# 374 kept rows instead of 372, the last folded group in two pieces of three rows, and a longer round through the small places

## The chip, the cores and the metric

The kernel runs on one core of one Trainium2 chip. The metric is the device time of one execution in microseconds (us); times are compared as medians of several runs on the same chip.

## The reference

The input `x` is an image of 384 x 384 pixels with 384 channels in bf16 (113.25 MB), `w1d` is a single weight. Each channel is averaged over all pixels, the average is weighted and goes through a sigmoid, and the whole image is multiplied by the result, channel by channel:

```python
B, H, W, C = x.shape
g = jnp.einsum("bhwc->bc", x) / (H * W)
s = jnp.zeros_like(g)
for i in range(k):                     # k = 1
    s = s + gp[:, i:i + C] * w1d[i]    # gp: g, padded by k // 2 = 0
s = _sigmoid(s)
return x * s[:, None, None, :]
```

All of `x` has to be read before the first element of the output is known, and all of it has to be written.

## The kernel before

**Rows and passes.** The image is seen as 128 partitions of 1152 rows; a row is one pixel's 384 channels in one partition, 768 bytes, so one row over all partitions is 98,304 bytes. The first pass (summing) loads all 1152 rows; TensorE multiplies each row by a matrix of ones and adds it to one PSUM bank, so that the bank holds the channels' sums in all partitions (`sum_rows`, L291). ScalarE makes the scale `s_bf` of it (L503) and puts a copy into the bank (L507, `s_ps`). The second pass (scaling) multiplies and stores all rows. A row that is still in SBUF then need not be read again. Rows that are not kept are called streamed: they are loaded, summed, and overwritten, and are loaded a second time for the scaling.

**Places.** SBUF holds an arena of 275 rows (`ROWS`). More rows than that are kept, by folding: four rows of bf16 values in the usual range of exponents fit into three. `fold` (L331) works on a piece of `p` rows of each of four parts: VectorE shifts and masks the fourth row's bits into temporary rows at `T` and joins them into free exponent bits of the other three; ScalarE looks at test values at `Y`, and records in `seen` whether a value was out of range (then GpSimd does those rows again at the end, `again`, L608). A group `(a, q)` holds 4q rows: 3q folded rows from `a` on, and behind them q "top" rows that become free when the group is folded. There is a first group of 4, two columns of four groups of eight, one group of six whose folded rows are copied into PSUM banks (`BANKED`), and a last one (`EXTRA`) of four at `A` (220). The rows that are kept unfolded ("raw") take the places that remain: the tops of the two columns' last groups (`U`, rows 108 to 115, and `V`, 212 to 219), the rows from `W` (232) on, and the rows `T` (259) and `Y` (267) to 274. `N_RAW`, `N_STREAM` and the runs of rows in DRAM follow from these (from L199 on).

**The summing pass.** A list (`BETWEEN`, L466) gives for each group which places the streamed rows between it and the next pass through. Large places of 48 rows come first; toward the end the places get smaller, since the arena fills with kept rows. Behind the last group, `EXTRA`, come four places of 8, 8, 8 and 7 rows (`LATE`, L465): `W + 4`, `U`, `W + 12`, `W + 20`, one load each. The raw rows come last (L495): `V`, again `LATE`, then `W`, `T`, `Y` in loads of 8 to 2 rows. A load into a place waits until TensorE has summed what was there. The number of rows in the second load of the whole pass is what the rest leaves over (`left % 48`, L474).

**Queues.** SyncE issues all loads and stores, in the order in which the program adds them; an issue waits for its semaphores, and everything behind it on SyncE waits with it. The transfers themselves are worked off in this order. `Flow` (L21) works out the waits. `hold` repeats a wait n times without work; `N_DVE` and `N_SP` (L371) say how often VectorE (at the start, and before the first scale) and SyncE do this.

**The scaling pass.** Its order is planned when the program is built, by a loop (L771) that plays VectorE and the queue through with assumed durations, and so decides which rows are scaled, stored, loaded and unfolded next. The places of raw rows are scaled first, in the order in which they stand in `landed` (L692 to L695); three pieces at the end of the rows behind `W` are scaled by GpSimd alongside (L701), and until GpSimd is thought to be done the planner starts no unfolding and lets VectorE read the scale from the bank. Then groups are unfolded in the order `order` (L707): per piece VectorE takes the fourth row's bits out (three `bits`, two `join`: L315, L321), restores the three rows, and scales. Rows whose store has landed become places for streamed rows.

Of the kernel before, what the change touches and what calls it, by code (L numbers as in the profile page):

```python
# [145 lines left out]
def kernel(  # L146
# [12 lines left out]
    P = nc.NUM_PARTITIONS  # L159
    B, H, W, C = x.shape  # L160
    (k,) = w1d.shape
    assert k == 1 and B == 1
    HW = H * W
    RPP = HW // P
# [7 lines left out]
    PIECE = 4  # L172
    PAIR = 2 * PIECE
    PAIRS = 4
    U = 3 * PIECE + PAIRS * 3 * PAIR
    G0 = U + PAIR
    V = G0 + PAIRS * 3 * PAIR
    A = V + PAIR
    N_A = 39
    T = A + N_A  # L180
    Y = T + 2 * PIECE
# [3 lines left out]
    FIRST = 0  # L185
    GROUPS = [(0, PIECE)]
    COLUMNS = ([FIRST], [])
    for i in range(PAIRS):
        for column, a in zip(COLUMNS, (3 * PIECE, G0)):
            column.append(len(GROUPS))  # L190
            GROUPS.append((a + 3 * PAIR * i, PAIR))
    BANKED = len(GROUPS)
    GROUPS.append((A, 6))
    EXTRA = len(GROUPS)
    GROUPS.append((A, PIECE))
    W = A + 3 * PIECE
    PS = 3 * GROUPS[BANKED][1]
    N_BANKED = 4 * GROUPS[BANKED][1] + 1
    N_RAW = ROWS - W + 2 * PAIR  # L199
    pool = ctx.enter_context(tc.tile_pool(name="sb", bufs=1))  # L200
# [1 line left out]

    pieces = [
        (g, lo, min(m, q - lo))
        for g, (_, q) in enumerate(GROUPS) for m in [q if g == BANKED else PIECE] for lo in range(0, q, m)
    ]

    ones = pool.tile([P, P], bf16, name="ones")
# [45 lines left out]
    for g, (_, q) in enumerate(GROUPS):  # L254
        c_group.append(N_STREAM if g == BANKED else r)
        r += 0 if g == BANKED else 4 * q
    c_raw = r
    assert c_raw + N_RAW == RPP

    def raw(a):  # L260

        return c_raw + (a - U if a < G0 else PAIR + a - V if a < A else 2 * PAIR + a - W)

# [3 lines left out]
    def load(at, a, n):  # L267

        r0, m = run = run_of(at)
        lo, hi = at - r0, at - r0 + n  # L270
        assert hi <= m
        fl.add(
            "SP",
            lambda: nc.sync.dma_start(out=arena[:, a : a + hi - lo, :], in_=view(xf, *run)[:, lo:hi, :]),  # L274
            writes=rows(a, hi - lo), dma=True,
        )
# [91 lines left out]
            join(w2, w2, flat(T + i * p, p), XOR, wc[2] + rows(T + i * p, p), wc[2])  # L368


    N_DVE, N_SP = (62, 14), 20  # L371

    fl.add("ACT", lambda: nc.scalar.dma_start(out=w_bf[:], in_=w1d.to_broadcast((1, 1))), writes=["w_bf"], dma=True)
    fl.add("DVE", lambda: nc.vector.memset(ones[:], 1.0), writes=["ones"])  # L374
# [25 lines left out]
    def stream_all(where, n=None):  # L400
        i = 0
        n = sum(m for _, m in where) if n is None else n
        while n:
            a, m = where[i % len(where)]
            m = min(n, m)
            stream(m, a)
            n -= m
            i += 1

    def take(g, lo=0, hi=None):  # L410

        a, q = GROUPS[g]
        hi = (N_BANKED if g == BANKED else 4 * q) if hi is None else hi
        load(c_group[g] + lo, a + lo, hi - lo)
        return sum_rows(a + lo, hi - lo)

    def of_group(g):
        return [i for i, piece in enumerate(pieces) if piece[0] == g]
# [13 lines left out]
    for i, bk in enumerate(banks):  # L432
        lo, hi = i * BANK, min((i + 1) * BANK, PS * C)
# [4 lines left out]
    S1, S2, S3 = ([slot] for slot in SLOTS)  # L438
# [9 lines left out]
    def group(g, where):  # L448

        if isinstance(where, list):  # L450
            take(g)
            for k in of_group(g):
                fold(k)
            stream_all(where)
        else:
            k1, k2 = of_group(g)
            take(g, 0, 12)
            take(g, 24, 32)
            fold(k1)
            stream_all(where[0])  # L460
            take(g, 12, 24)
            fold(k2)
            stream_all(where[1])

    LATE = [(W + 4, 8), (U, 8), (W + 12, 8), (W + 20, 7)]  # L465
    BETWEEN = [  # L466
        (2, LOW_COLUMN + HIGH), (4, [(A, 38)]),
        (5, [(G0 - 24, 24), (A - 24, 24), *S1]),
        (6, (S2, S3 + S1)), (7, ([(A - 24, 24)] + S2, S3 + S1)),
        (8, (S2 + S1, [(U, 8)] + S3)), (EXTRA, LATE),  # L470
    ]
    between = sum(n for _, b in BETWEEN for w in b for _, n in (w if isinstance(w, list) else [w]))
    first = N_STREAM - between
# [18 lines left out]
        load(raw(a), a, n)  # L492
        return sum_rows(a, n)

    for a, n in [(V, 8), *LATE, (W, 4), (T, 4), (T + 4, 4), (Y, 4), (Y + 4, 2), (Y + 6, 2)]:  # L495
        step = take_raw(a, n)
        if a == Y - 4:
            fl.hold("DVE", 2 * N_DVE[1], step)
# [144 lines left out]
    landed = deque()  # L643
# [45 lines left out]
        return f  # L689


    for a, n, end in ((Y, 2, True), (Y + 2, 2, True), (Y + 4, 4, True), (U, 4, True), (U + 4, 4, True), (T, 8, True), (V, 8, True)):  # L692
        landed.append((a, raw(a), n, end))
    landed.append((W, raw(W), 8, True))
    landed.append((W + 8, raw(W + 8), 6, True))  # L695


    alongside = deque()
    t = 1.0
    for a, n in ((A + 26, 4), (A + 30, 4), (A + 34, 5)):  # L700
        scale(a, n, "POOL", after=[copied])  # L701
        t += 0.2 + 0.84 * n
        alongside.append((t, a, raw(a), n))


    (c0, c1), N_NEAR = COLUMNS, 2
    order = [c0[-1], EXTRA, c0[-2], c1[-1], BANKED, c0[-3], c1[-2], c0[-4], c1[-3], FIRST, c1[-4]]  # L707
    line = deque(order)
    home = {g: i for i, column in enumerate(COLUMNS) for g in column}
    home[BANKED], home[EXTRA] = 2, 3  # L710
# [60 lines left out]
    while True:  # L771

        if dve_at <= now:
# [4 lines left out]
            if landed and (ahead < PENDING or not can):  # L778
                a, at, n, end = landed.popleft()
# [13 lines left out]
        if alongside and alongside[0][0] <= now:  # L793
            _, a, at, n = alongside.popleft()
# [3 lines left out]
        while waiting and waiting[0][0] <= now:  # L798
            _, n, then, at, a, known = waiting.popleft()
# [10 lines left out]
        if bank_at is None and len(line) <= total - BANKS_AT and got and max(got)[0] >= N_BANKED:  # L810
            a = max(got)[1]
# [3 lines left out]
            for i, bk in enumerate(banks):  # L815
                lo, hi = i * BANK, min((i + 1) * BANK, PS * C)
# [6 lines left out]
        if got and todo < N_STREAM:  # L823
            n, a = max(got)
            left = N_STREAM - todo
            left -= run_of(left - 1)[0]
            n = min(n, CAP, left)
            ahead = backlog()
            behind = storing and sum(m for m, _ in got) < MANY and ahead >= SHORT
            if not behind and (todo or not (landed or alongside or waiting)) and (n >= min(BIG, left) and (n == left or left > CAP) or (ahead < LOW and n >= 8) or ahead < LAST):  # L830
                storing = False

                lo = N_STREAM - todo - n
# [51 lines left out]
```

## Time and profile before

| | us |
|---|---|
| median of 3 runs | 719.24 |
| lowest and highest | 718.77, 719.40 |
| the profiled execution's own time | 718.83 |
| its span, first to last instruction | 717.1 |

The page shows one execution. Its engines: TensorE busy 213.0 us, VectorE 475.2, ScalarE 121.4, GpSimd 10.2. In the fences, PE is TensorE, DVE VectorE, ACT ScalarE, POOL GpSimd, SP SyncE (SPq its issues of transfers); L517 is a line of the kernel. In a view in order of time, a row has the start, the duration, the engine, the line, the operation with its shape, how often it stands there, and in brackets the idle time before it and what ended that. In the views of transfers stand the size of one and the median time from issue to landing, so a wait in the queue is part of it. The summing pass ends near 268 us, and the first store is issued at 269.8.

### The profile page before, as it was taken

How to read it: one execution, taken by the hardware profiler on the slowest of the kernel's cores; microseconds unless marked ns; L12 is line 12 of the kernel's file. 1: busy time of each engine (PE TensorE's matmuls, PEld its weight loads, DVE VectorE, ACT ScalarE, POOL GpSimd, SP SyncE). 2: the span in 40 equal slices, each digit the busy share in tenths (PEclk: the TensorE clock that was granted, in tenths of full speed). 3: DMA queues.
4: the chain of work that ended last, by engine and by line, in shares of the span. 5: the costliest groups of instructions: out<-in, count | busy, mean ns of one | idle time of the engine just before them, and what ended most of it. 6: DMA issues, size and time to landing. Idle time of an engine off the chain costs nothing.

```text
span 717.1 us, 2040 instructions
## 1 busy us (share of the span) xinstructions
PE 213.0 (30%) x1186; PEld 0.3 (0%) x3; DVE 475.2 (66%) x355; ACT 121.4 (17%) x97; POOL 10.2 (1%) x7
## 2 busy tenths in 40 slices
PE   4776978998869780000000000000000000000000
PEld 0000000000000000000000000000000000000000
DVE  4606280639896829999999999779966960128900
ACT  3704160426674610000110000000000000000000
POOL 0000000000000005000000000000000000000000
PEclk9998989999999996555555555555555555555555
DMA  9999999999999989999999999999999999999997
GB/s 373 436 426 440 424 442 426 439 429 420 428 430 425 427 358 355 406 424 431 433 428 422 444 424 445 423 439 428 439 420 435 433 433 436 436 432 431 437 421 343
DMA packets 21038, 303.31 MB, mean 423 GB/s; under 512 B 2338, under 2 KB 2850, under 8 KB 9378
## 3 DMA queue, kind: packets, MB, share of 16 engines
q1 hardware_dynamic: 21024, 303.18, 99.1%
q8 instruction: 4, 0.07, 0.0%
q14 instruction: 8, 0.07, 0.0%
q10 hardware_dynamic: 2, 0.00, 0.0%
HBM read 189.92 MB, written 113.25 MB: 423 GB/s over the span
## 4 chain that ended last, share of the span: by engine, by line
DMA 56%; DVE 23%; PE 7%; another core or an unknown queue 3%; ACT 2%; POOL 1%; SPq 1%; issue 0%; DVEq 0%
DMA arena<-in_x_dram 45%; DVE arena L517 17%; DMA out_dram<-arena 11%; PE bank L280 7%; DVE arena L315 4%; ACT arena L352 2%; DVE arena L321 2%; POOL arena L517 1%; SPq L274 1%; SPq L531 0%; ACT s_bf L503 0%; ACT bank L507 0%; ACT bank L429 0%; DVEq L124 0%
## 5 line engine op out<-in xcount | busy, mean ns | idle before, releaser
L517 DVE TENSOR_TENSOR arena<-arena,s_bf 128x6144 bf16<-128x6144 bf16 (+13 forms) x67 | 226.9, 3424 | 86.1 <-DMA arena<-in_x_dram 71.0
L280 PE MATMUL bank<-arena,ones 128*128 128x384 bf16 x1151 | 207.2, 342 | 46.2 <-DMA arena<-in_x_dram 45.6
L315 DVE TENSOR_SCALAR arena<-arena 128x1536 uint16<-128x1536 uint16 (+4 forms) x193 | 136.9, 763 | 107.6 <-DMA arena<-in_x_dram 94.9
L352 ACT ACTIVATE arena<-arena 128x3072 uint16<-128x3072 uint16 (+1 forms) x38 | 107.6, 2831 | 111.6 <-DVE arena L315 111.6
L321 DVE TENSOR_TENSOR arena<-arena 128x1536 uint16<-128x1536 uint16 (+3 forms) x81 | 106.3, 1312 | 8.4 <-PE bank L280 5.2
L597 PE MATMUL bank<-odd,ones 128*128 128x1 bf16 x1 | 0.2, 184 | 262.2 <-DVE odd L592 262.2
L429 ACT COPY arena<-bank 128x512 uint32<-128x512 uint32 (+3 forms) x9 | 4.4, 497 | 86.6 <-DMA out_dram<-arena 86.3
L517 POOL TENSOR_TENSOR arena<-arena,s_bf 128x1536 bf16<-128x1536 bf16 (+1 forms) x3 | 9.9, 3345 | 269.2 <-ACT bank L507 269.2
L517 DVE TENSOR_TENSOR arena<-arena,bank 128x1536 bf16<-128x1536 bf16 (+3 forms) x8 | 9.4, 1248 | 0.0
L429 ACT COPY bank<-arena 128x512 uint32<-128x512 uint32 (+3 forms) x9 | 4.1, 489 | 26.5 <-PE bank L280 26.5
L352 ACT ACTIVATION_READ_ACCUMULATOR arena<-arena 128x1 f32 x38 | 7.1, 186 | 0.0
L280 PE MATMUL bank<-zeros,ones 128*128 128x384 bf16 x32 | 5.5, 326 | 0.0
L503 ACT ACTIVATE s_bf<-bank,w_sc 128x384 bf16<-128x384 f32 x1 | 0.6, 580 | 13.6 <-PE bank L280 13.6
L294 PE MATMUL bank<-arena,ones 128*128 128x384 bf16 x1 | 0.5, 477 | 7.1 <-DMA arena<-in_x_dram 7.1
L853 ACT ACT_TABLE_LOAD x1 | 1.3, 1283 | 0.7 <-PEq L869 0.7
L384 DVE TENSOR_SCALAR w_sc<-bank 128x1 f32<-128x1 f32 x1 | 0.2, 159 | 1.4 <-PE bank L379 1.4
L379 PE MATMUL bank<-w_bf,ones 1*128 1x1 bf16 x1 | 0.2, 183 | 2.4 <-DMA w_bf<-in_w1d_dram 2.4
L374 DVE MEMSET ones<- 128x128 bf16 x1 | 0.2, 165 | 1.0 <-SPq L118 1.0
L601 DVE CAST odd_i<-bank 128x1 int32<-128x1 f32 x1 | 0.2, 159 | 0.3 <-PE bank L597 0.3
L507 ACT COPY bank<-s_bf 128x192 uint32<-128x192 uint32 x1 | 0.3, 323 | 0.0
L597 PEld LDWEIGHTS bank<-odd,ones 128*128 128x128 bf16 x1 | 0.1, 102 | 521.0 <-DVE odd L592 521.0
L587 DVE TENSOR_REDUCE worst<-seen 128x1 f32<-128x38 f32 x1 | 0.2, 184 | 0.0
(8 smaller groups left out, 0.9 us busy)
## 6 DMA issues: line engine op xcount, KB each, us to landing
arena<-in_x_dram SPq DMA_DIRECT2D x18, 4608.0 KB, 31.8
out_dram<-arena SPq DMA_DIRECT2D x9, 4608.0 KB, 34.5
out_dram<-arena SPq DMA_DIRECT2D x7, 3072.0 KB, 23.6
arena<-in_x_dram SPq DMA_DIRECT2D x5, 3072.0 KB, 15.2
arena<-in_x_dram SPq DMA_DIRECT2D x13, 1152.0 KB, 17.1
arena<-in_x_dram SPq DMA_DIRECT2D x6, 2304.0 KB, 20.1
arena<-in_x_dram SPq DMA_DIRECT2D x15, 768.0 KB, 7.7
arena<-in_x_dram SPq DMA_DIRECT2D x2, 4128.0 KB, 38.2
```

The costliest lines, as they stand in the source:

```text
L274: lambda: nc.sync.dma_start(out=arena[:, a : a + hi - lo, :], in_=view(xf, *run)[:, lo:hi, :]),
L280: return pe.add_instruction(mybir.InstMatmult(name=nc.get_next_instruction_name(), ins=[pe.lower_ap(rhs), pe.lower_ap(ones[:])], outs=[pe. ...
L294: return nc.tensor.matmul(acc, lhsT=ones[:], rhs=arena[:, i, :], start=first, stop=last)
L315: lambda: nc.vector.tensor_scalar(out=dst, in0=src, scalar1=s0, scalar2=s1, op0=op0, op1=op1),
L321: "DVE", lambda: nc.vector.tensor_tensor(out=dst, in0=a, in1=b, op=op), reads=reads, writes=writes
L352: lambda: nc.scalar.activation(out=y, in_=y, func=ACTF.Copy, accum_out=seen[:, 2 * k + i : 2 * k + i + 1]),
L429: "ACT", lambda: nc.scalar.copy(dst.bitcast(u32), src.bitcast(u32)), reads=reads, writes=writes
L503: lambda: nc.scalar.activation(out=s_bf[:], in_=acc, func=ACTF.Sigmoid, scale=w_sc[:, 0:1]),
L507: "ACT", lambda: nc.scalar.copy(s_ps.bitcast(u32), s_bf[:].bitcast(u32)), reads=["s_bf"], writes=["bank0"]
L517: lambda: vec.tensor_tensor(out=v, in0=v, in1=s[:, None, :].to_broadcast([P, n, C]), op=Op.mult),
L597: lambda: nc.tensor.matmul(votes, lhsT=ones[:], rhs=odd[:], start=True, stop=True),
L853: nc.scalar.preload_act_table(ACTF.Sigmoid)
```

## The change

The last folded group, `EXTRA`, gets six rows instead of four; it is loaded and folded in two pieces of three rows. It takes 18 folded rows and six tops, so `W` moves from 232 to 238, six fewer rows are kept raw, eight more folded, and two fewer are streamed. `LATE` loses the place `W + 4`. Between the group's two halves eight streamed rows pass through `U`; behind the second pass `W + 6` (8), `W + 14` (7), `V` (8), and `LATE` once more. The raw rows behind `W` are loaded as four and two. GpSimd's three pieces become five rows each, the order in which landed rows are scaled is changed, and `EXTRA` comes third in the unfolding instead of second. VectorE's wait at the start is repeated less often.

```diff
+    LAST_GROUP = 6
     BANKED = len(GROUPS)
     GROUPS.append((A, 6))
     EXTRA = len(GROUPS)
-    GROUPS.append((A, PIECE))
-    W = A + 3 * PIECE
+    GROUPS.append((A, LAST_GROUP))
+    W = A + 3 * LAST_GROUP
...
-        for g, (_, q) in enumerate(GROUPS) for m in [q if g == BANKED else PIECE] for lo in range(0, q, m)
+        for g, (_, q) in enumerate(GROUPS) for m in [{BANKED: q, EXTRA: q // 2}.get(g, PIECE)] for lo in range(0, q, m)
...
-    N_DVE, N_SP = (62, 14), 20
+    N_DVE, N_SP = (50, 14), 20
...
             k1, k2 = of_group(g)
-            take(g, 0, 12)
-            take(g, 24, 32)
+            q = GROUPS[g][1]
+            take(g, 0, 3 * q // 2)
+            take(g, 3 * q, 4 * q)
             fold(k1)
             stream_all(where[0])
-            take(g, 12, 24)
+            take(g, 3 * q // 2, 3 * q)
             fold(k2)
             stream_all(where[1])
 
-    LATE = [(W + 4, 8), (U, 8), (W + 12, 8), (W + 20, 7)]
+    LATE = [(U, 8), (W + 6, 8), (W + 14, 7)]
...
-        (8, (S2 + S1, [(U, 8)] + S3)), (EXTRA, LATE),
+        (8, (S2 + S1, [(U, 8)] + S3)), (EXTRA, (LATE[:1], LATE[1:] + [(V, 8)] + LATE)),
...
-    for a, n in [(V, 8), *LATE, (W, 4), (T, 4), (T + 4, 4), (Y, 4), (Y + 4, 2), (Y + 6, 2)]:
+    for a, n in [(V, 8), *LATE, (W, 4), (W + 4, 2), (T, 4), (T + 4, 4), (Y, 4), (Y + 4, 2), (Y + 6, 2)]:
...
-    for a, n, end in ((Y, 2, True), (Y + 2, 2, True), (Y + 4, 4, True), (U, 4, True), (U + 4, 4, True), (T, 8, True), (V, 8, True)):
+    for a, n, end in ((Y, 2, True), (Y + 2, 2, True), (Y + 4, 4, True), (W, 4, True), (W + 4, 2, True), (T, 8, True), (U, 8, True)):
         landed.append((a, raw(a), n, end))
-    landed.append((W, raw(W), 8, True))
-    landed.append((W + 8, raw(W + 8), 6, True))
+    landed.append((V, raw(V), 8, True))
...
-    for a, n in ((A + 26, 4), (A + 30, 4), (A + 34, 5)):
+    for a, n in ((A + 24, 5), (A + 29, 5), (A + 34, 5)):
...
-    order = [c0[-1], EXTRA, c0[-2], c1[-1], BANKED, c0[-3], c1[-2], c0[-4], c1[-3], FIRST, c1[-4]]
+    order = [c0[-1], c0[-2], EXTRA, c1[-1], BANKED, c0[-3], c1[-2], c0[-4], c1[-3], FIRST, c1[-4]]
```

## The prediction

> **What bounds the kernel now.** I read the page first (span, the 40 slices, the queues, the chain), then the engines in stretches, then SyncE's waits, then the order of time around the turn from the summing pass to the scaling pass.
>
> ```profile
> span 717.1 us, 2040 instructions
> DMA  9999999999999989999999999999999999999997
> GB/s 373 436 426 440 424 442 426 439 429 420 428 430 425 427 358 355 406 424 431 433 428 422 444 424 445 423 439 428 439 420 435 433 433 436 436 432 431 437 421 343
> q1 hardware_dynamic: 21024, 303.18, 99.1%
> HBM read 189.92 MB, written 113.25 MB: 423 GB/s over the span
> ```
>
> One queue, SyncE's, moves everything, and its packets fill 99.1% of sixteen engines' time. The kernel is bound by bytes, except in three places: the first slice, slices 14 to 16, and the last slice. A change can win by moving fewer bytes or by closing those holes; it can lose by opening a new one or by moving the same bytes in dearer pieces. The read bytes show what is kept: 189.92 - 113.25 = 76.67 MB are read a second time, which at 98,304 bytes a row (128 partitions x 384 x 2) is 780 rows; 372 are kept.
>
> The second view gives busy time of each engine by stretch (us from the start; the last three columns are TensorE's granted clock, DMA share and GB/s).
>
> ```profile
> 100.00:150.00 50.00, 45.91 (x253) 0.00 (x0) 19.63 (x27) 15.71 (x14) 0.00 (x0) 0.91 1.00 431
> 245.00:255.00 10.00, 8.36 (x51) 0.00 (x0) 8.58 (x12) 6.97 (x6) 0.00 (x0) 1.00 1.00 420
> 255.00:262.00 7.00, 5.28 (x30) 0.00 (x0) 0.00 (x0) 0.00 (x0) 0.00 (x0) 1.00 1.02 422
> 262.00:269.00 7.00, 6.08 (x35) 0.00 (x0) 0.00 (x0) 0.41 (x1) 0.00 (x0) 1.00 0.64 253
> 269.00:280.00 11.00, 0.00 (x0) 0.00 (x0) 10.80 (x11) 0.49 (x2) 9.95 (x3) 0.67 0.85 344
> 280.00:290.00 10.00, 0.00 (x0) 0.00 (x0) 9.81 (x10) 0.00 (x0) 0.00 (x0) 0.50 1.02 395
> 290.00:300.00 10.00, 0.00 (x0) 0.00 (x0) 9.90 (x9) 0.00 (x0) 0.00 (x0) 0.50 1.00 392
> 320.00:400.00 80.00, 0.00 (x0) 0.00 (x0) 79.25 (x45) 4.37 (x9) 0.00 (x0) 0.50 1.01 429
> 420.00:700.00 280.00, 0.18 (x1) 0.10 (x1) 181.88 (x65) 0.00 (x0) 0.00 (x0) 0.50 1.00 432
> ```
>
> Three prices are in it. A row of large transfers costs 98,304 B / 432 GB/s = 0.2276 us. Eight-row transfers (245 to 262) run at 420 to 422: 786,432 B take 1.864 to 1.872 us where 431 would give 1.825, so a further transfer costs about 0.04 us more than its bytes. And in the stretches shown from 269 to 400 VectorE is busy 98% and more: there the two are nearly level, and what VectorE loses can reach the queue.
>
> **What is removed, added and moved.** Counted in the order in which each program issues them:
>
> - Streamed rows 780 to 778: two rows are not read again.
> - Summing pass: 58 loads become 63, still 1152 rows. The second load shrinks from 30 rows to 5 (the 25 rows now stand at the end), the last folded group is loaded as 9 + 6 and 9 rows instead of 16, and 46 streamed rows in 7- and 8-row loads follow its second half where 31 did.
> - Scaling pass: 88 transfers become 94, 1932 rows become 1930; transfers of at most 12 rows go from 41 to 49, those of 5 or 10 rows from 11 to 23.
> - VectorE folds two pieces of three rows instead of one of four, unfolds them in two pieces, and waits 50 times instead of 62 (each a double wait) at the start.
> - GpSimd scales 5+5+5 rows instead of 4+4+5; VectorE scales 38 landed rows instead of 46 before its first unfolding.
>
> **The queue's own sum.** Two rows less: -2 x 0.2276 = -0.46 us. Eleven transfers more: +11 x 0.04 = +0.44. Together 0.0. The ends: the 0.04 could be nothing (-0.46), or all of what the worst rows show (280 to 300, 393 GB/s, so 2.00 us for eight rows and 0.175 above their bytes: +1.93 - 0.46 = +1.5). I take 0.04, since the loads of 7 and 8 rows are the nearest to what is added; the far end is a rival below. The Trainium skill, page "DMA: Bandwidth & Descriptors", section on the anatomy of one DMA, gives each transfer a fixed cost of about 2.0 us beside its bytes. Were it paid one after another, eleven more would cost 22 us and the time would be 741; the trace's 0.04 leaves that no chance, since the next transfer already stands in the queue.
>
> **The folds.** Quoted in order of time, with the idle time before and what ended it in brackets:
>
> ```profile
> 247.11 6.95 PE L280 MATMUL bank<-arena,ones 128*128 128x384 bf16 x40 [1.28 <-DMA arena<-in_x_dram]
> 247.16 1.90 DVE L315 TENSOR_SCALAR arena<-arena 128x3072 uint16<-128x3072 uint16 x3 [1.00 <-DMA arena<-in_x_dram]
> 252.93 1.95 DVE L321 TENSOR_TENSOR arena<-arena 128x1536 uint16<-128x1536 uint16 x2
> 256.14 1.46 PE L280 MATMUL bank<-arena,ones 128*128 128x384 bf16 x8 [0.56 <-DMA arena<-in_x_dram]
> 266.16 2.40 PE L280 MATMUL bank<-arena,ones 128*128 128x384 bf16 x12 [0.20 <-DMA arena<-in_x_dram]
> 268.59 0.58 ACT L503 ACTIVATE s_bf<-bank,w_sc 128x384 bf16<-128x384 f32 x1 [13.62 <-PE bank L280]
> 269.61 9.95 POOL L517 TENSOR_TENSOR arena<-arena,s_bf 128x1536 bf16<-128x1536 bf16 x3 [269.16 <-ACT bank L507]
> 269.79 11.04 SPq L531 DMA_DIRECT2D out_dram<-arena  x12
> ```
>
> The last fold runs from 247.16 to 254.88, 7.7 us for four rows, and VectorE then does nothing until the scale is there. Three rows cost at most that; two pieces, 15.4 us at most. Its loads come 25 x 0.2276 = 5.7 us earlier, so both are done by about 257, with 12 us of idle VectorE before 269.2 as the cover. Uncovered, they would hold back the reload of the group's own top rows, which is the seventh last load but none of the first. The 12 waits dropped at the start fall into this idle time, so they cost nothing:
>
> ```profile
> 9.61 2.70 DVE L315 TENSOR_SCALAR arena<-arena 128x4608 uint16<-128x4608 uint16 x3 [6.80 <-DMA arena<-in_x_dram]
> 23.23 13.70 PE L280 MATMUL bank<-arena,ones 128*128 128x384 bf16 x73 [4.88 <-DMA arena<-in_x_dram]
> 32.09 18.71 SPq L274 DMA_DIRECT2D arena<-in_x_dram  x4
> ```
>
> **Two places where the queue gets shorter.** (1) The load issued at 32.09 waits for the sum of 43 rows. Two loads stand before it now, 30 and 48 rows; with 5 the queue behind the first 84 rows (which land when PE starts at 23.2) ends at 23.2 + 53 x 0.2276 = 35.3, so 3.2 us stand ahead of it. (2) The small places at the end hold 31 rows where the last rounds before had 39 (the place of eight behind the group's top is gone). A place is free about 1.55 us after its load landed (1.46 for its eight sums), and 23 rows stand ahead in the other places: 5.3 - 1.55 = 3.75 us. What a load needs between issue and its first byte:
>
> ```profile
> 305.86 6.24 DMA arena<-in_x_dram
> 0.96 49.84 SPq L274 DMA_DIRECT2D arena<-in_x_dram  x9
> ```
>
> The first is a ten-row load from the chain of waits: 6.24 - 2.3 of its own = 3.9 us were enough. The very first load, issued at 0.96 into an empty queue, let VectorE start at 9.61: 25 rows are 5.7 us, so 2.95 at a cold start. The need lies below 3.9 and is about 3.0 or less, so I take both places at nothing; were it 3.9, the first would lose 0.7 and each of the two and a half rounds at the end some 0.2 to 0.9, about 2 us.
>
> **The turn.** Sum, scale, first store and first store's landing keep their steps. After it the change meets a lock:
>
> ```profile
> 274.40 4.68 DVE L517 TENSOR_TENSOR arena<-arena,bank 128x3072 bf16<-128x3072 bf16 x3
> 275.73 3.83 POOL L517 TENSOR_TENSOR arena<-arena,s_bf 128x1920 bf16<-128x1920 bf16 x1
> 278.99 1.93 DVE L315 TENSOR_SCALAR arena<-arena 128x1536 uint16<-128x1536 uint16 x3
> 286.80 5.28 SPq L531 DMA_DIRECT2D out_dram<-arena  x3
> 291.63 1.49 DVE L315 TENSOR_SCALAR arena<-arena 128x1536 uint16<-128x1536 uint16 x3
> out_dram<-arena SPq DMA_DIRECT2D x1, 1152.0 KB, 8.9
> out_dram<-arena SPq DMA_DIRECT2D x2, 192.0 KB, 1.9
> ```
>
> Three field operations took 1.93 us at 278.99 and 1.49 at 291.63: the first began while GpSimd ran on until 279.56 (275.73 + 3.83), and lost 0.44 of the 0.56 us that they overlapped. The scales before it, which read the scale from the bank, kept their pace beside GpSimd (4.68 for three). I take it that VectorE waits for GpSimd's end. In the changed program GpSimd's three pieces of five rows (3.83 each) end at 269.6 + 11.4 = 281.0, and VectorE is free 8 rows earlier, at about 277.3, where it must also wait for the landing of the 8 rows stored from place U, near 279.8. So its first unfolding begins at 281.0 and not 279.56: 1.45 us late. Behind it on VectorE stand the scales of all landed rows, and on SyncE the 12-row store issued at 286.80 (the 1152 KB row of the transfers from 280 to 300: 8.9 us to landing, of which 2.7 are its own, so 6.2 of queue). The new order puts 3 rows fewer before it, 0.7 us; 6.2 - 1.45 - 0.7 = 4.0 us of queue are left as cover, and a store needs some 1.45 (two-row stores into an empty queue, last row: 1.9 less 0.45 of their own). GpSimd's last store is issued 1.4 us later, and the first reload after it on SyncE too, behind 59 rows then and 53 now. I cost both at nothing. Uncovered, each us late on VectorE is a us of queue.
>
> **Sum.** -0.46 + 0.44 + 0 = 0.0 on the span of 717.1; the profiled execution's own time is 718.83, 1.7 more than its span, and the median of the runs is 719.24, 0.4 above that. I add 0.1 for the places with thin cover and put it on the median: 719.3 to 719.4.
>
> **Rivals.**
>
> - Price of pieces. Two spells are slow inside full queues, in half-us slices of 280 to 300:
>
> ```profile
> GB/s 492 418 393 393 455 415 424 398 261 215 201 384 442 418 418 430 442 406 442 445 369 292 184 307 381 498 369 498 350 461 369 442 442 393 406 442 430 386 422 409
> ```
>
> At 284 to 285.5 and 290.5 to 292 the rate halves: (430-226)/430 x 1.5 + (430-261)/430 x 1.5 = 1.3 us. Both fall on transfers of 5 and 10 rows; but most of the eleven such transfers ran at line. If the spells belong to them, 23 instead of 11 make 2.7 us, 1.4 more: 720.7 to 720.8.
> - The other side: the load's need. Place: the four small places and the load at 32.09. It decides from 3.2 us between issue and first byte; at 3.9 it costs 2 us, 721.3. Against it: the cold start's 2.95. SyncE's waits for PE in the summing pass would grow together with idle DMA.
> - The lock costs more, the queue runs dry at the first unfolded store: 4.0 us of cover would have to go; then about 1 us, 720.3.
> - The two slow spells were that execution's own or go with the old order: -1.3, 718.0.
>
> **How the numbers follow.** Forecast 0.58 (own range 718.8 to 719.9); pieces 0.18; load's need 0.13; lock 0.04; spells gone 0.07. A measurement of this kernel tells about 0.2% (1.44 us) from no change: below 717.8 faster, above 720.7 slower. Faster: more than half of the last case, 0.05. Slower: most of the pieces (0.12), of the load's need (0.10) and a little of the lock: 0.23. Within: 0.72. The range holds all but the far ends of both sides: 718.1 to 721.2.
>
> **What would show it.** Right: read 189.72 MB; DMA share 1.00 to 1.02 from 25 to 262 and from 300 on; the first field operation about 1.5 us late and GpSimd's last end at 281; the first store within 0.4 us of 269.8. Wrong: a dip of the DMA share near 35 or 245 to 262 (the load's need), slow half-us slices at every 5-row and 10-row transfer (pieces), a hole at 289 to 292 with SyncE waiting for VectorE (lock), or a time beyond the range from a place not named here.

## The result and the profile after

The changed kernel takes 724.72 us (median of six runs, 722.63 to 725.94), the kernel before on the same chip 719.29 us (six runs, 718.21 to 719.67): 1.0076 times as long, 95% interval 1.0056 to 1.0096. It is slower by 5.4 us. The profiled execution took 725.84 us, 7.0 more than that of before, and the same 7.0 more in its span. Two stray executions further down (992 us in run 13, 1634 us in run 16) are in no ratio.

The page of the changed kernel, the lines that correspond to those of before (span, share and rate of the DMA engines in 40 slices, the one queue, the bytes):

```profile
span 724.1 us, 2075 instructions
DMA  9999999999999997999999999999999999999997
GB/s 375 427 399 442 434 432 433 423 416 424 428 429 422 412 366 298 392 408 426 428 431 425 431 443 422 436 432 439 425 438 422 443 429 439 432 434 426 438 429 319
q1 hardware_dynamic: 22608, 302.98, 98.8%
HBM read 189.73 MB, written 113.25 MB: 418 GB/s over the span
```

The bytes are those predicted (two rows less), and the time is longer all the same. The third slice has fallen from 426 to 399 GB/s, the sixteenth from 355 to 298. The stretches below are cut around these slices (the last three columns: TensorE's granted clock, DMA share, GB/s). First the changed kernel:

```profile
30.00:40.00 10.00, 7.98 (x50) 0.00 (x0) 2.25 (x3) 2.38 (x2) 0.00 (x0) 1.00 0.96 372
245.00:252.00 7.00, 5.51 (x32) 0.00 (x0) 6.59 (x11) 5.28 (x5) 0.00 (x0) 1.00 1.01 422
252.00:262.00 10.00, 6.52 (x37) 0.00 (x0) 3.61 (x7) 2.88 (x4) 0.00 (x0) 1.00 0.94 339
288.00:298.00 10.00, 0.00 (x0) 0.00 (x0) 8.79 (x6) 0.00 (x0) 0.00 (x0) 0.50 0.92 318
420.00:700.00 280.00, 0.18 (x1) 0.10 (x1) 200.84 (x77) 0.00 (x0) 0.00 (x0) 0.50 1.01 433
```

The kernel before, at the same three places (its first store is issued 4.6 us earlier):

```profile
30.00:40.00 10.00, 6.93 (x43) 0.00 (x0) 1.84 (x3) 1.97 (x2) 0.00 (x0) 1.00 1.04 450
252.00:262.00 10.00, 7.92 (x44) 0.00 (x0) 2.84 (x5) 2.86 (x2) 0.00 (x0) 1.00 1.02 423
284.00:294.00 10.00, 0.00 (x0) 0.00 (x0) 9.85 (x10) 0.00 (x0) 0.00 (x0) 0.50 1.01 370
```

There are three dips, at 30 to 40, 252 to 262 and 288 to 298, and nothing in the long scaling stretch (433 GB/s against 432). In each, the share of busy DMA engines falls by 0.08 to 0.09 against before, but the rate by 14 to 20%: there are gaps, and in the time that packets do run they move 6 to 13% fewer bytes.

For a single transfer I call "loss" the time from the landing before it to its own, less what its rows take in a full queue (0.2267 us a row and 0.08; most transfers come out between -0.1 and 0 by this). "Queue ahead", or lead, is the time from its issue to the landing before it. Both come from the issues and landings; below stand the start of the issue, then KB of one transfer and us from issue to landing. The load that the kernel before issues at 32.09, in the changed kernel:

```profile
32.63 1.28 SPq L275 DMA_DIRECT2D arena<-in_x_dram  x3
```

```profile
arena<-in_x_dram SPq DMA_DIRECT2D x1, 4608.0 KB, 15.9
```

and in the kernel before:

```profile
arena<-in_x_dram SPq DMA_DIRECT2D x1, 4608.0 KB, 19.6
```

Its 48 rows take 10.96 us. Before, 19.6 - 10.96 = 8.6 us; the landing before it comes 8.8 us after its issue, so all of this is the queue ahead, and the loss is nothing. After, 15.9 - 10.96 = 4.94 us, of which 2.76 are queue: 2.2 us lost. At the small places the same sum gives 1.45 us over three loads with 3.7 to 4.3 us ahead (before: none). At the first reloads of the scaling pass 3.35 us are lost over four transfers, before 1.3: 2.0 more. Together 2.2 + 1.45 + 2.0 = 5.7 of the 7.0 us; 0.3 are the first load's, and the remaining 1.0 is the balance of many small differences.

Not every loss comes with a short queue. In the kernel before, the 32-row load issued at 32.46, right behind the one above, took

```profile
arena<-in_x_dram SPq DMA_DIRECT2D x1, 3072.0 KB, 27.9
```

of which 19.3 us are queue and 7.3 its rows: 1.3 lost with a full queue ahead. In the changed kernel a 48-row load issued at 85.6 lost 1.4 with 21.0 ahead. The trace has an instruction fetch of 16,384 bytes, 0.95 us long, among the packets of each (at 55.8 and 110.3), and the last few packets of that load still run when packets of the next load have begun more than a microsecond before. These two losses cancel between the kernels; later fetches of the same size cost nothing (162.2 and 217.7 in the kernel before), and why is not shown.

The third place in detail. The half-microsecond slices of the changed kernel from 280 to 300:

```profile
GB/s 481 406 393 406 467 455 430 406 393 406 467 395 415 399 422 392 121 68 135 220 253 338 389 326 301 416 387 378 402 384 301 292 359 378 464 439 436 422 433 447
```

Stores up to 288, then 2 us at some 140 GB/s, then 7 us of reads at some 350 before the full rate is reached at 297.

The turn itself, in order of time:

```profile
273.22 0.58 ACT L505 ACTIVATE s_bf<-bank,w_sc 128x384 bf16<-128x384 f32 x1 [17.44 <-PE bank L281]
274.23 11.39 POOL L519 TENSOR_TENSOR arena<-arena,s_bf 128x1920 bf16<-128x1920 bf16 x3 [273.79 <-ACT bank L509]
274.42 11.57 SPq L533 DMA_DIRECT2D out_dram<-arena  x11
284.38 2.60 DVE L316 TENSOR_SCALAR arena<-arena 128x1536 uint16<-128x1536 uint16 x3 [2.34 <-DMA out_dram<-arena]
```

GpSimd ends at 285.62, 11.4 us after it began, as predicted. VectorE's first three field operations take 2.60 us where 1.49 is their undisturbed time: 1.1 lost of the 1.24 us that they lie beside GpSimd. The lock is there, and what waits behind it had cover (the 12-row store of unfolded rows still had 5.9 us of queue ahead).

### The profile page after: what moved, and what is told of

Its sections match the earlier page's. It is cut to its first block, busy times and chain, and to the rows that moved or that the text cites. A ratio compares the mean times of both kernels' runs of the same rounds, so it can differ in the third digit from the quotient of the medians.

```text
span 724.1 us, 2075 instructions
## 1 busy us (share of the span) xinstructions
PE 214.0 (30%) x1186; PEld 0.3 (0%) x3; DVE 484.3 (67%) x384; ACT 124.6 (17%) x101; POOL 11.6 (2%) x7
## 3 DMA queue, kind: packets, MB, share of 16 engines
HBM read 189.73 MB, written 113.25 MB: 418 GB/s over the span
## 4 chain that ended last, share of the span: by engine, by line
DMA 66%; DVE 18%; PE 7%; ACT 2%; POOL 2%; SPq 1%; issue 0%; DVEq 0%
DMA arena<-in_x_dram 49%; DMA out_dram<-arena 17%; DVE arena L519 13%; PE bank L281 7%; DVE arena L316 4%; ACT arena L353 2%; DVE arena L322 2%; POOL arena L519 2%; SPq L275 1%; SPq L533 0%; ACT s_bf L505 0%; ACT bank L509 0%; ACT bank L430 0%; DVEq L124 0%; SPq L881 0%
## 5 line engine op out<-in xcount | busy, mean ns | idle before, releaser
L519 DVE TENSOR_TENSOR arena<-arena,s_bf 128x6144 bf16<-128x6144 bf16 (+14 forms) x73 | 229.0, 3171 | 95.8 <-DMA arena<-in_x_dram 76.8
L316 DVE TENSOR_SCALAR arena<-arena 128x1536 uint16<-128x1536 uint16 (+6 forms) x210 | 142.3, 731 | 102.6 <-DMA arena<-in_x_dram 90.1
L353 ACT ACTIVATE arena<-arena 128x3072 uint16<-128x3072 uint16 (+2 forms) x40 | 110.5, 2763 | 107.8 <-DVE arena L316 107.8
L322 DVE TENSOR_TENSOR arena<-arena 128x1536 uint16<-128x1536 uint16 (+4 forms) x88 | 109.8, 1247 | 10.2 <-PE bank L281 6.9
L519 POOL TENSOR_TENSOR arena<-arena,s_bf 128x1920 bf16<-128x1920 bf16 x3 | 11.4, 3827 | 273.8 <-ACT bank L509 273.8
L519 DVE TENSOR_TENSOR arena<-arena,bank 128x3072 bf16<-128x3072 bf16 (+2 forms) x7 | 7.7, 1175 | 0.0
```

What stands on the lines that cost most here:

```text
L316: lambda: nc.vector.tensor_scalar(out=dst, in0=src, scalar1=s0, scalar2=s1, op0=op0, op1=op1),
L322: "DVE", lambda: nc.vector.tensor_tensor(out=dst, in0=a, in1=b, op=op), reads=reads, writes=writes
L353: lambda: nc.scalar.activation(out=y, in_=y, func=ACTF.Copy, accum_out=seen[:, 2 * k + i : 2 * k + i + 1]),
L519: lambda: vec.tensor_tensor(out=v, in0=v, in1=s[:, None, :].to_broadcast([P, n, C]), op=Op.mult),
```

## The experiments

Six theories. A: a load issued with too little queue ahead finds its first packets slow (near the prediction's second rival, the load's need). B: more and smaller transfers cost (its first, the price of pieces). C: instruction fetches take the DMA engines' time. E: the new order of places and rows makes the reads slow. D and G come up on the way. All ratios are to the kernel before on the same chip, with 95% intervals; they go by means, the times given beside them are medians. Losses and leads stand for the one execution of each run that was profiled.

### The load early in the summing pass

**Run 2: the changed kernel with the short streamed load in fourth place.** The load that takes what is left over is the second of the streamed loads and the fourth of the whole pass, not its second as "The summing pass" has it; here it becomes the fourth streamed one.

```diff
-    sizes = [N_FIRST] + [left % 48] * (left % 48 > 0) + [48] * (left // 48)
+    sizes = [N_FIRST] + [48] * (left // 48)
+    sizes.insert(3, left % 48)
```

> The changed kernel, with the load of 5 streamed rows issued as the fourth of the large streamed loads and not as the second, so that the load that waits for the sum of the first 43 rows again has 96 rows (some 12 us) of queue ahead of it and not 53 rows (2.8 us). Rows, sizes and number of transfers stay. Theory A: the 2.2 us that the landings lose at that load are gone, median 722.0 to 723.0 against 724.7. Theory B: no change from the changed kernel, 724 to 725. Theory C: no change there either.

722.25 us, ratio 1.0042 (1.0026 to 1.0059). The stretch is back:

```profile
30.00:40.00 10.00, 7.95 (x50) 0.00 (x0) 1.86 (x3) 1.99 (x2) 0.00 (x0) 1.00 1.02 442
```

With 12 us of queue or more in front of every load there the 2.2 us are gone, and the median is 2.5 us lower. In two other profiles of kernels that keep the short load second (runs 3 and 4) the long load behind it lost 0.9 and 0.7, so this loss varies from one execution to the next. That fits the spread of the changed kernel's six runs.

### The small places

**Run 1: the kernel before with 31 rows in the last round through the small places (the ring) instead of 39.** `V` is loaded later, so that four places carry the round.

```diff
-    for a, n in [(V, 8), *LATE, (W, 4), ...
+    for a, n in [*LATE, (V, 8), (W, 4), ...
```

> The kernel before, with one thing moved: in the raw loads at the end, the eight rows of place V are loaded after the four places behind them and not ahead of them. Rows, sizes and number of transfers stay. The load of W+4 then follows 31 rows after the load that it replaces, not 39, so only some 2.8 us of queue stand ahead of it (4.9 before). Theory A (a load needs about 5 us of queue ahead of it, or its first packets are slow): the queue's landings fall back by 1 to 2.5 us between 252 and 262, and the median is 720.3 to 721.8. Theory B (more and smaller transfers cost the time) and theory C (the instruction fetches of SyncE and TensorE hit the queue): no change, 719.0 to 719.6.

720.74 us, ratio 1.0023 (1.0013 to 1.0033): slower by 1.6 us by the ratio, with not one transfer more. Of two 8-row loads with 3.0 and 3.6 us ahead the first lost nothing, the second 1.3 us; it landed at 259.9, and the next instruction fetch came at 261.1, so C has no part in it:

```profile
252.00:262.00 10.00, 6.92 (x39) 0.00 (x0) 3.46 (x6) 2.86 (x2) 0.00 (x0) 1.00 0.97 357
```

**Run 7: run 2, and loads of three and four rows in these places.**

```diff
-    LATE = [(U, 8), (W + 6, 8), (W + 14, 7)]
+    LATE = [(U, 4), (U + 4, 4), (W + 6, 4), (W + 10, 4), (W + 14, 4), (W + 18, 3)]
```

(and `V` in two halves.)

> As the second run (short load in fourth place, 722.25 us), and the 46 streamed rows behind the last folded group and the 31 raw rows after them pass through the small places in loads of three and four rows instead of seven and eight: 11 transfers more, but a place is free again after four sums, so about 5 us of queue stand ahead of each load where 3.8 did. Theory A (short queue ahead): the dip at the small places (1.0 to 1.45 us) goes, against 11 x 0.04 = 0.44 us for the further transfers: 721.2 to 721.7 us, and the DMA share from 248 to 262 back to 1.00. Theory B (the smaller transfers are what costs): the loss there grows instead, 723 us or more.

721.69 us, ratio 1.0033 (1.0021 to 1.0045). The stretch of run 2, then of run 7:

```profile
250.00:260.00 10.00, 6.92 (x40) 0.00 (x0) 2.92 (x6) 2.22 (x2) 0.00 (x0) 1.00 0.95 356
```

```profile
250.00:260.00 10.00, 8.56 (x43) 0.00 (x0) 2.92 (x6) 2.22 (x2) 0.00 (x0) 1.00 1.03 414
```

Eleven transfers more did not make the kernel slower: the median is 0.6 us lower, though the two intervals overlap, and the 1.0 us that run 2's profile lost at these places is gone. B, which expected 723 or more, has the wrong sign. A gave the time here; 1.0 - 0.6 leaves some 0.4 us for the eleven transfers, 0.04 each.

**Run 4: the changed kernel with `N_SP` 15 instead of 20.**

> The changed kernel, with SyncE's repeated waits cut from 20 double ones to 15, so that its first store stands at the same place of its program as in the kernel before and its instruction fetch falls into the pause before the first store instead of into the small places' loads (256.9, 1.06 us long). Theory C: the loss of 1.45 us at the loads that land at 257 to 262 goes, median 723 to 723.6. Theory A: that loss stays, since these loads keep 3.7 to 4.3 us of queue ahead, and the median stays at 724 to 725. Theory B: no change.

722.70 us, ratio 1.0066 (1.0042 to 1.0091), from 721.9 to 726.5. The instruction fetch that fell into the dip at 257 (1.06 us long) moved to 263, and the ring lost 0.4 us instead of 1.45; but the load of the first place also lost less in this profile. By run 1 the ring's loss needs no fetch, and no fetch lies in the other two dips of the changed kernel (none between 17.0 and 52.6, none between 273.7 and 425.6). Whether the one at 257 added to the dip there stays open.

### The first reloads of the scaling pass

**Run 3: the changed kernel with GpSimd's pieces 4+4+5 as before.**

> The changed kernel, with GpSimd scaling 4, 4 and 5 rows as before instead of 5, 5 and 5, and VectorE the two rows more. GpSimd's end and the first reload behind it on SyncE come some 1.4 us earlier, so the first reload has about 4.2 us of queue ahead instead of 3.0. Theory A: the loss at the first reloads (2.8 us in the changed kernel against 1.4 in the kernel before) falls to about 1 us, median 722.7 to 724. Theory B: the transfers are 95 instead of 94 in the second pass, so no gain, 724.5 to 725. Theory C: no change.

725.71 us, ratio 1.0095 (1.0079 to 1.0112): no gain and above the range of every theory, though the first reload had 4.8 us of queue ahead instead of 3.0. It lost 1.3 us instead of 2.3, and the third reload, with 7.0 ahead, lost 1.9.

**Runs 5 and 6: the distance between partitions in DRAM (theory D).** `N_FIRST` 45 in the kernel before, 41 in run 2's kernel.

> The kernel before with its first load of 45 rows instead of 43, which leaves 735 rows in the long streamed run, the same distance between two partitions in DRAM as in the changed kernel (735 x 768 B), where the kernel before has 737. Nothing else moves: same number of transfers, same queue ahead of each. Theory D (the distance between partitions makes the first reloads of the scaling pass slow): the loss at the first three reloads rises from about 1.4 us to about 3.3 us, time about 721.2 us, ratio 1.002 to 1.003. Theory A (only a queue too short ahead of a load) and theory B (smaller transfers): no change, 719.0 to 719.6 us.

> The changed kernel with the short load of the stream moved to fourth place (as in the second run: 722.25 us) and its first load of 41 rows instead of 43, so that the long streamed run has 737 rows as in the kernel before; the short load has 7 rows instead of 5. Theory D (distance between partitions): the first reloads lose about 1.4 us instead of 3.4, time about 720.3 us. Theories A and B: unchanged, 721.8 to 722.7 us.

719.85 (ratio 1.0011, 1.0002 to 1.0020) and 722.10 us (1.0039, 1.0026 to 1.0053). The losses at the reloads stayed with the kernel and not with the distance: D falls.

**Run 8: the kernel before with GpSimd's pieces 5+5+5.**

> The kernel before with GpSimd's three pieces of 5+5+5 rows in place of 4+4+5, as in the changed kernel; the landed rows that VectorE scales first are two fewer. GpSimd ends about 1.7 us later, and about 4.3 us of queue stand ahead of the first reload where 5.3 did. If the 5+5+5 pieces and the later, thinner queue make the first reloads slow (theory A for this place), their loss rises from 1.4 to about 2.5 to 3.3 us: 720.3 to 721.2 us. Theory D (distance between partitions) and B: 719.0 to 719.6 us.

720.06 us, ratio 1.0010 (1.0001 to 1.0019), between the ranges of A and of no change. The first reload, with 4.5 us ahead, lost 1.9 us.

**Runs 9, 10, 11: more queue ahead of the first reload, in run 7's kernel.** GpSimd with two pieces instead of three; the first reload allowed out ahead of GpSimd's third store; pieces 4+4+5.

> The seventh run's kernel (721.69 us) with GpSimd scaling two pieces of five rows instead of three; the third piece of five goes to VectorE, behind the landed rows. No store of GpSimd's then stands between SyncE's queue and the first reloads, and each of these goes out with about 5 us of queue or more ahead, where the first had 3.1. Theory A (a load issued with too little queue ahead): the loss at the first reloads falls from about 3.4 us to 1.4 or less, as in the kernel before, and one transfer more may cost 0.04: 719.5 to 720.2 us. If something else in the new order of places and rows makes these reads slow (theory E: the reads themselves, whatever their lead): 721.3 to 722.0 us.

> The seventh run's kernel (721.69 us) with the rule dropped that no reload is issued while a GpSimd store is outstanding: the first reload (11 rows) goes out ahead of GpSimd's third store, about 4.7 us of queue ahead of it instead of 3.1, and SyncE's order changes behind it (one of the next reloads gets about 3.1 us). Theory A: the loss of the first reload falls from about 2.0 to 2.4 us to under 1.3, the later short one may take part of it back: 720.2 to 721.4 us. Theory E: no change, 721.4 to 722.0 us.

> The seventh run's kernel (721.69 us) with GpSimd's pieces of 4+4+5 rows as in the kernel before. In the third run this change alone brought nothing (725.71 us), though the first reload had 4.8 us of queue ahead instead of 3.0. Here the other two dips are gone, so the reload stage is seen alone. Theory A: loss at the first reloads 1.4 to 2.5 us instead of 3.4, 719.8 to 720.9 us. Theory E: the loss there stays at 3.4 to 4.0 us, 721.4 to 722.3 us.

724.47 (1.0080, 1.0067 to 1.0093), 725.55 (1.0090, 1.0076 to 1.0103), 723.16 us (1.0063, 1.0050 to 1.0076). All three are slower than run 7, and all three lie above the ranges of A and of E. In runs 9 and 10 the first reload did lose less (1.1 and 0.9 instead of 2.0), but the edits moved the transfers behind it, and later loads lost more: in run 10 one issued at 333 with 1.1 us ahead lost 1.8; in run 9 four with 5 to 8 us ahead lost 0.8 to 1.3 each, for which no run shows the cause. In run 11, 2.1 were lost in spite of 4.8 us ahead.

**Runs 12 and 13: only the first reload later, in the kernel before.**

```diff
+    LATER = -2
...
-                load(lo, a, n)
+                load(lo, a, n, [f for f in fl.steps if f.eng == "DVE"][LATER:] [:1] if todo == 0 else ())
```

(run 13: `LATER = -1`; `load` hands the steps on as waits.)

> The kernel before, in which only the first reload of the scaling pass (8 rows, issued at 280.88 with 5.35 us of queue ahead) has one more wait: for VectorE's second join, which ends at about 282.9. So about 3.3 us of queue stand ahead of it, as in the changed kernel (3.0 to 3.1); the load behind it goes out 0.8 us later, nothing else moves, and the queue is not empty at any time. Theory A (lead): the first reload loses 1.5 to 2.4 us where it lost none, time 720.6 to 721.5 us. Theory E (the new order of places and rows makes the reads slow, not their lead): 718.9 to 719.5 us.

> As the run before, but the added wait is for VectorE's next operation, which ends at about 284.2: about 2.0 us of queue ahead of the first reload. Theory A: a larger loss, 2.5 to 3.7 us, time 721.6 to 722.8 us. Theory E: 718.9 to 719.7 us.

722.02 us, ratio 1.0043 (1.0030 to 1.0057), and 719.31 us, ratio 1.0004 (0.9994 to 1.0013). With less ahead (2.6 us) the run was no longer than before, though the reload itself lost 0.5; with more (4.2) it was 2.8 us longer. At this place the lead alone does not decide: A, which expected 721.6 to 722.8 for run 13, falls here.

What seems to set the profiles apart is how soon SyncE issues the reload behind the store before it. **Theory G:** issued within half a microsecond of that store, it pays.

**Runs 14 and 15: lead and closeness parted.** Run 14 is run 7 with about 1 us of waiting between the store and the first reload. Run 15 is the kernel before with the wait put ahead of the store.

```diff
+                if todo == 0:
+                    fl.hold("SP", 40, copied)
                 load(lo, a, n)
```

> The seventh run's kernel (721.69 us) with SyncE made to wait some 1.1 us between GpSimd's third store and the first reload (11 rows): about 2 us of queue ahead of it instead of 3.1, but the issue no longer follows the store's at 0.45 us. Theory A (lead alone): the first reload loses more, 2.6 us or more instead of 2.0, time 722.2 to 723.2 us. Theory G (a load whose issue follows another issue at under half a microsecond is prepared late, and this is what the first reloads of the changed kernel pay): the loss falls to about 0.5 to 1.0 us, 720.2 to 721.0 us.

> The kernel before with SyncE made to wait some 1.3 us ahead of GpSimd's third store, so that the first reload follows that store at about 0.45 us instead of 1.3; its queue ahead stays at about 5 us (5.35 before). Theory A: no loss at the first reload, 719.0 to 719.6 us. Theory G: it loses 1.3 to 2.0 us, 720.4 to 721.2 us.

720.20 us, ratio 1.0013 (1.0004 to 1.0023): 1.5 us faster than run 7, by making SyncE wait. And 722.14 us, ratio 1.0042 (1.0029 to 1.0056): 2.6 us slower than before with the lead nearly kept, more than G's 721.2. E falls with these two: run 14 keeps the new order of places and rows and wins most of the time back, run 15 keeps the old order and loses as much. Issues and landings of store and reload, run 7:

```profile
281.81 0.33 SPq L534 DMA_DIRECT2D out_dram<-arena  x1
282.27 0.38 SPq L275 DMA_DIRECT2D arena<-in_x_dram  x1
```

```profile
arena<-in_x_dram SPq DMA_DIRECT2D x1, 1056.0 KB, 7.7
out_dram<-arena SPq DMA_DIRECT2D x1, 480.0 KB, 3.5
```

Run 14:

```profile
281.88 0.33 SPq L534 DMA_DIRECT2D out_dram<-arena  x1
283.54 0.34 SPq L275 DMA_DIRECT2D arena<-in_x_dram  x1
```

```profile
arena<-in_x_dram SPq DMA_DIRECT2D x1, 1056.0 KB, 5.0
out_dram<-arena SPq DMA_DIRECT2D x1, 480.0 KB, 2.9
```

The load goes out 1.27 us later and lands at 288.5 instead of 290.0; the store too lands earlier (284.8 instead of 285.3). The slices from 280 to 300, run 7, then run 14:

```profile
GB/s 467 442 442 337 438 415 423 330 200 114 169 287 203 338 363 332 290 346 370 372 427 359 335 246 307 313 449 430 436 442 406 430 442 372 459 439 386 450 399 422
```

```profile
GB/s 393 430 442 392 399 438 407 445 192 237 118 287 389 473 372 410 393 442 442 449 384 461 415 310 289 458 424 387 498 364 465 406 422 456 396 396 418 455 446 412
```

Both have much the same hole from 284 to 286. In run 14 the rate is back at 286; in run 7 it stays at some 340 until 293. What run 7 loses beyond run 14 is thus not the hole but the slow packets behind it. The load of run 14 had 1.2 us of queue ahead, and 5.0 us from issue to landing are 2.5 more than its bytes. In the trace its first packets start at 284.5, 1.0 us after the issue and 0.1 behind the last of the store; the first fifteen take 0.55 to 1.5 us each, where its later ones take 0.32. So the hole is made of slow packets as well as of gaps. The Trainium skill, page "DMA: Bandwidth & Descriptors", section "Specifications", gives about 0.6 us to the first byte of such a transfer; the 1.0 us of this trace does not test it, since the store's packets ran until 0.1 us before.

Run 15, where the reload of the kernel before got the closeness:

```profile
281.33 0.33 SPq L531 DMA_DIRECT2D out_dram<-arena  x1
281.72 1.26 SPq L274 DMA_DIRECT2D arena<-in_x_dram  x1
```

```profile
arena<-in_x_dram SPq DMA_DIRECT2D x1, 768.0 KB, 8.3
out_dram<-arena SPq DMA_DIRECT2D x1, 480.0 KB, 5.2
```

The store lands at 286.5 and the reload, 1.8 us of bytes, at 290.0. In the kernel before they landed at 286.2 and 288.1:

```profile
280.88 1.23 SPq L274 DMA_DIRECT2D arena<-in_x_dram  x1
```

```profile
arena<-in_x_dram SPq DMA_DIRECT2D x1, 768.0 KB, 7.2
...
out_dram<-arena SPq DMA_DIRECT2D x1, 480.0 KB, 6.6
```

**Runs 16, 17, 18: G elsewhere.** The same wait in run 2's kernel, in run 11's, and a longer one in the kernel before.

> The second run's kernel (the changed kernel with its short streamed load in fourth place, 722.25 us) with SyncE made to wait some 1.1 us ahead of the first reload, as in the fourteenth run; the small places keep their loads of seven and eight rows. Theory G (closeness to the store before it): 1.5 us less, as from the seventh to the fourteenth run, 720.5 to 721.1 us, with the dip at the small places still there. If the gain of the fourteenth run hung on the smaller loads: 721.8 to 722.6 us.

> The eleventh run's kernel (GpSimd's pieces 4+4+5, 723.16 us), where the first reload had 4.8 us of queue ahead, followed a store by 0.46 us, and still lost 2.1 us; here with the 1.1 us wait of SyncE ahead of it: 3.7 us ahead, 1.5 us behind the store. Theory G: 720.8 to 722.0 us. Theory A: 723.0 to 724.5 us. Theory E (the order of places and rows): 722.8 to 723.6 us.

> The kernel before with SyncE made to wait some 3 us ahead of the first reload, which goes out at about 282.7 to 283.2, as in the twelfth and the thirteenth run, but without a wait for VectorE: 2.5 to 3.5 us of queue ahead, over 3 us behind the store. Theory G: no more than 0.7 us lost, 719.0 to 719.9 us. Theory A: 720.6 to 722.0 us. If the twelfth run's 722.0 us comes from the moment of the issue, this one shows it too; if from its tie to VectorE, it does not.

720.58 us, ratio 1.0015 (1.0005 to 1.0024): 1.7 less than run 2, as G says. 722.08 us, ratio 1.0037 (1.0023 to 1.0051): 1.1 less than run 11 (1.9 by the ratios, the chips differ), just above G's range (720.8 to 722.0), and two later reloads with 5.3 and 6.7 us ahead still lost 1.5 each. 719.95 us, ratio 1.0013 (1.0002 to 1.0023): 0.4 more than before, just above G's 719.9; the wait was longer than meant, and only 1.0 us stood ahead.

The profiles side by side (us; losses are those of the store before the first reload and of that reload):

| kernel | reload behind store | queue ahead | store lost | reload lost |
|---|---|---|---|---|
| before | 1.3 | 5.3 | 0.7 | 0.0 |
| changed | 0.45 | 3.0 | 0.5 | 2.3 |
| 3 | 0.45 | 4.8 | 0.8 | 1.3 |
| 7 | 0.46 | 3.1 | 0.6 | 2.0 |
| 8 | 0.48 | 4.5 | 0.7 | 1.9 |
| 9 | 1.3 | 4.9 | 0.9 | 1.1 |
| 10 | 0.9 | 4.8 | 0.8 | 0.9 |
| 11 | 0.46 | 4.8 | 0.9 | 2.1 |
| 12 | 2.4 | 4.2 | 0.7 | 0.9 |
| 13 | 3.4 | 2.6 | 0.2 | 0.5 |
| 14 | 1.7 | 1.2 | 0.0 | 1.3 |
| 15 | 0.4 | 4.9 | 0.8 | 1.6 |
| 16 | 1.7 | 1.2 | 0.0 | 1.1 |
| 17 | 1.7 | 2.9 | 0.2 | 1.6 |
| 18 | 4.7 | 1.0 | 0.0 | 1.3 |

Store and reload together lose 2.1 to 3.0 us in all six kernels where the reload follows within half a microsecond, and 0.7 to 2.0 in the nine others. Runs 2, 4 and 6, not in the table, go with the six (0.45 us behind, 3.1 ahead, 2.7 to 3.0 lost), runs 1 and 5 with the kernel before (1.3 behind, 5.3 ahead, 0.5 to 0.6 lost). The gap between the two sets is thin: run 9 lost 2.0 at a distance of 1.3 us, run 3 lost 2.1 at 0.45. **What stays open:** why closeness should matter, and whether it is closeness itself or something that goes with it; run 12, whose 2.8 us lie only for a part at this place (the third reload lost 1.6 us, 0.65 before, and later ones some); and the losses of 0.5 to 1.5 us that single loads with 5 us and more ahead show in runs 9, 11 and 17. Run 15 too lost 3.3 us at two later reloads with 3.7 to 4.0 us ahead, which lost nothing in the kernel before with the same lead; its store and first reload account for 1.7 us more than before, so its 2.6 us can't be put down to closeness alone.

## Why the prediction was wrong

The forecast was 719.3 to 719.4 us, the range 718.1 to 721.2; the measured 724.72 lies beyond both, and beyond every rival. The sign that the prediction gave for the load's need, a dip of the DMA share near 35 or from 245 to 262, appeared at both places.

- **The queue's own sum (0.0): right.** 189.73 MB are read, the long stretch runs at 433 GB/s, and in run 7 eleven further small transfers cost some 0.4 us where the prediction had 0.44 for as many. "Price of pieces" was no case: in the changed kernel's scaling pass the 23 transfers of 5 and 10 rows lost 1.7 us in all, the 11 of the kernel before 1.1. The 2.0 us for each transfer that the prediction quotes from the Trainium skill, page "DMA: Bandwidth & Descriptors", section on the anatomy of one DMA, stand there for transfers that GpSimd issues; here SyncE issues. The 0.04 us are the price behind a full queue and no other.
- **The folds: right.** Both pieces lie in VectorE's idle time; no dip comes from them (run 7 has the second fold in the same stretch, 2.92 us of VectorE from 250 to 260 as in run 2, and no dip).
- **"Two places where the queue gets shorter": the step that failed.** The prediction named both places, worked out 3.2 and 3.75 us of queue, and then took them at nothing ("The need lies below 3.9 and is about 3.0 or less, so I take both places at nothing"). They cost 2.2 and 1.45 us in the profile, 2.5 by run 2 and 1.6 by run 1's parallel in the kernel before. The bound was read from two loads that happened to lose nothing: one ten-row load with 3.9 us, which at the same lead lost 0.9 us in the changed kernel's profile and 1.7 in run 15, and the cold start. A single case without a loss bounds no need. The rival "load's need" had the place and the condition; its 2 us were half of the price, since it counted a gap alone, and the packets behind the gap are slow as well.
- **The turn: lock right, reload wrong.** GpSimd's end, the slowed field operations and the cover of the unfolded store came as worked out. "GpSimd's last store is issued 1.4 us later, and the first reload after it on SyncE too ... I cost both at nothing" failed. The reload left 0.45 us behind that store with 3.0 us of queue ahead, and the stage lost 2.0 us more than before. Run 16 gives 1.7 of them back by a wait alone; that the place of the issue costs is shown by this, the mechanism behind it is not.
- **The sum of what the runs took back:** by the ratios 5.5 us slower for the changed kernel, 3.0 for run 2, 1.1 for run 16, 0.9 for run 14. The 0.9 hold the 22 further transfers less two rows (22 x 0.04 - 0.46 = 0.4). No variant beat the kernel before; what the change itself can gain, two rows, is 0.46 us.

## What to carry to other kernels

On a queue that is full 99% of the time, this change cost what it did to the queue ahead of the loads issued into its thin places, not what it did to bytes. For such a kernel list every load with less than about 5 us ahead before and after, and put a range from nothing to 2 us on each rather than a yes or no from one load that got away. Where reads start again behind stores, look at when the first one is issued: in this kernel waiting about a microsecond was faster than issuing at once. Judge such an edit by the whole run and not by the one load it was meant for, since moving the order shifts the losses to others (runs 9 and 10).

## What the runs showed of the hardware that was not expected

- Loads with 2.0 to 3.2 us of queue ahead lost 0.7 to 2.2 us (48 rows), with 3.0 to 4.3 none to 1.3 (7 and 8 rows, ring), and with 5 or more in the same ring nothing. The loss is in part a gap and in part slow packets behind it: at the small places the DMA share fell by 0.08 where the rate fell by a fifth, at the first reloads by 0.09 where the rate fell by 14%.
- A reload about 0.45 us behind a store lost 1.3 to 2.4 us with 3.0 to 4.9 us ahead; about a microsecond of waiting, which left 1.2 us ahead, saved 1.5 to 1.7 us of the run (runs 14 and 16). The store before a close reload lost 0.5 to 0.9 us, but so did the store in runs 9, 10, 12 and the kernel before, where the reload came 0.9 to 2.4 us later (0.7 to 0.9); with the wait, in runs 14 and 16, the store lost nothing.
- In a full queue a load lost 1.3 us (kernel before, 19.3 us ahead) and 1.4 us (changed kernel, 21.0 ahead) where an instruction fetch of 16,384 bytes, 0.95 us long, ran among its packets.
- The dose did not go one way: with 4.2 us ahead 722.0 us, with 2.6 us 719.3 us, with 1.0 us 720.0 us (runs 12, 13, 18).
